# Two tiles of layer two's first chunk take their denominators by tokens, and two chunks' sums of phi(K) leave TensorE

## The chip, the cores and the metric

The kernel runs on one core of one Trainium2 chip. The metric is the device time of one execution in microseconds. The engines are TensorE (PE, with its weight loads as PEld), VectorE (DVE), ScalarE (ACT), GpSimd (POOL) and SyncE (SP), which only issues DMAs. Each engine works through its own instructions in order and waits for the others by semaphores.

## The reference

Two layers of the same weights: linear attention and an MLP, each behind a layer norm and with a residual. There are 2048 tokens of 512 values, 32 heads of 16 values, and 1792 hidden values.

```python
def _A_ref(x, wqkv, wo):
    qkv = (x @ wqkv) ...            # q, k, v: heads x tokens x 16
    phi = lambda t: jnp.where(t > 0, t + 1, jnp.exp(t)) + 1e-6
    pq, pk = phi(q), phi(k)
    kv = jnp.einsum("bhsd,bhse->bhde", pk, v)
    z = jnp.einsum("bhsd->bhd", pk)
    num = jnp.einsum("bhqd,bhde->bhqe", pq, kv)
    den = jnp.einsum("bhqd,bhd->bhq", pq, z)[..., None] + 1e-6
    return (num / den)... @ wo
def _B_ref(x, w1, b1, w2, b2):
    return _gelu(_layernorm(x) @ w1 + b1) @ w2 + b2
x = A_x
x = x + _A_ref(_layernorm(x)); x = x + _B_ref(x)
x = x + _A_ref(_layernorm(x)); x = x + _B_ref(x)
```

## The kernel before

The tokens are cut into 4 chunks of 512, and each chunk into 4 tiles of 128 tokens (tile numbers 0 to 15). Names of operations end in layer, chunk or tile, and part: `K0_5` is the K projection of tile 5 in layer one, `Q1_0_2` the Q projection of chunk 0, part 2, in layer two.

Per tile: `stats`, `aggr`, `veps`, `pow` and `norm` make the layer norm (`A` before the attention, `B` before the MLP), a DMA transpose issued by SP (`TA`, `TB`) turns it, and `K` projects it. `exp`, `relu`, `min` and `phi` are the four steps of phi: two on ScalarE, `min` on VectorE, the last addition on VectorE or GpSimd. `G` collects y^T phi(K) over the tokens (y being the normed input; four PSUM banks are held for it in layer one, `gacc` adds chunks up in layer two). `KV` multiplies that by Wv, `kvm` masks it to the diagonal blocks of the heads, `M` multiplies by Wo, and `cpm` copies the result to `gtb`, the matrix that `WO` uses. Then come `RA` (residual), the second norm, `W1` with the gelu, `W2`, and `RB` (residual) or the output `OD`. `b2` adds the MLP's bias to the residual beside that.

In layer one tiles 0 to 3 are turned by TensorE (`PTC0`, `PTC1`, `PTA0_2`, `PTA0_3`, copied by ScalarE as `tcC`, `tcA`). In the first microseconds TensorE runs filler matmuls (`warm`).

The sum z of phi(K) over all tokens is made in two ways in `attn_z`. One takes 16 matmuls of one column per chunk (`Z0_c`, L970; `zs` adds them up). The other, used for the first three chunks of layer two, adds the tiles' phi(K) elementwise in fp32 (`za`, L958), splits the sum into two bf16 halves (`zhi`, `zlo`) and sums each over the tokens with four matmuls of one column (`ZH`, L933 and L934; `zsh` takes the result).

The denominators are made in two ways in `attn_den`. By features: Q is made with features on the partitions, `D` (L1100) multiplies it by `zb` (z on the heads' diagonal blocks), ScalarE takes Ln and Exp(-x) (L1102, L1104) and `pr` multiplies (L1108). By tokens: Q is made with tokens on the partitions, `pz` multiplies by the row of z (L1077), `red` sums per head (L1080), `den` adds 1e-6 (L1083, 128x32 values), `rec` is the reciprocal (L1085), `pr` multiplies (L1089), and a DMA transpose `TP` (L1093) turns the result. Chunk 0 of each layer goes by features, the others by tokens.

The order on every engine is written out by name in `CONF["ORDER"]`, the buffers in `PLACES`, and in `WAY` which engine does a step that several can do. `LOADS` gives the first loads and their queues. There is no scheduler at run time: each engine takes its list from first to last.

Of the kernel before, what the change touches and what calls it, by code (L numbers as in the profile page):

```python
# [1359 lines left out]
```

## Time and profile before

| | us |
|---|---|
| median of 3 runs | 323.17 (322.78 to 323.9) |
| the profiled execution | 323.1 |
| its span, first to last instruction | 321.9 |
| busy: PE, DVE, ACT, POOL | 318.0, 218.1, 189.3, 145.5 |
| granted TensorE clock | 1.000 |

Lines of a timeline read: start in us, length in us, engine, line of the source, operation, output <- input, shape, how many were merged, and in brackets the idle time of the engine before it and what ended that. Lines of waits read: who waited <- for whom: us in total, times, longest. Groups read: busy us, mean ns of one | idle before. Lines of one source line read: shortest/median/longest in ns, first and last start. DMA lines read: how many, (KB each,) median us from issue to landing. Rows of windows read: stretch and its length, then busy us (count) of PE, PEld, DVE, ACT and POOL, granted clock, DMA share and GB/s.

### The profile page before, as it was taken

How to read it: one execution, taken by the hardware profiler on the slowest of the kernel's cores; microseconds unless marked ns; L12 is line 12 of the kernel's file. 1: busy time of each engine (PE TensorE's matmuls, PEld its weight loads, DVE VectorE, ACT ScalarE, POOL GpSimd, SP SyncE). 2: the span in 40 equal slices, each digit the busy share in tenths (PEclk: the TensorE clock that was granted, in tenths of full speed). 3: DMA queues.
4: the chain of work that ended last, by engine and by line, in shares of the span. 5: the costliest groups of instructions: out<-in, count | busy, mean ns of one | idle time of the engine just before them, and what ended most of it. 6: DMA issues, size and time to landing. Idle time of an engine off the chain costs nothing.

```text
span 321.9 us, 4748 instructions
## 1 busy us (share of the span) xinstructions
PE 318.0 (99%) x1703; PEld 157.4 (49%) x1703; DVE 218.1 (68%) x529; ACT 189.3 (59%) x324; POOL 145.5 (45%) x216
## 2 busy tenths in 40 slices
PE   8999999999999999999999999999999999999997
PEld 3444554666444444444444444558544444444444
DVE  5998789999786774028848899999889881101103
ACT  5898656797730636667962367979634442663320
POOL 6573978688655355101822415887454163000000
DMA  7844793142121412111010200122232322201002
GB/s 257 200 81 85 241 348 85 35 82 36 33 49 34 82 33 51 34 33 32 18 40 10 51 16 0 35 51 52 50 62 54 98 65 67 49 0 35 16 33 65
DMA packets 52355, 21.68 MB, mean 67 GB/s; under 512 B 47532, under 2 KB 50860, under 8 KB 52332
## 3 DMA queue, kind: packets, MB, share of 16 engines
q1 hardware_dynamic: 50844, 16.37, 22.4%
q0 software_dynamic: 1056, 4.72, 4.3%
q10 hardware_dynamic: 432, 0.30, 0.3%
q8 instruction: 13, 0.21, 0.3%
q14 instruction: 10, 0.08, 0.1%
HBM read 8.00 MB, written 2.10 MB: 31 GB/s over the span
## 4 chain that ended last, share of the span: by engine, by line
PE 97%; DMA 2%; DVE 0%; issue 0%
PE ps L1153 30%; PE ps L1190 29%; PE ps L1123 9%; PE ps L879 8%; PE ps L896 6%; PE ps L984 4%; PE ps L1013 4%; DMA t<-in_A_x_dram 2%; PE ps L909 2%; PE ps L1176 1%; PE ps L970 1%; PE ps L1034 1%; PE ps L1057 1%; PE ps L1100 1%; DVE stats L775 0%; PE ps L1048 0%
## 5 line engine op out<-in xcount | busy, mean ns | idle before, releaser
L1158 ACT ACTIVATE gT<-ps,b1c 128x512 bf16<-128x512 f32 (+1 forms) x140 | 77.0, 601 | 68.7 <-PE ps L1153 68.1
L1153 PE MATMUL ps<-t,w 128*128 128x512 bf16 (+1 forms) x560 | 102.5, 336 | 0.0
L1190 PE MATMUL ps<-w,gT 128*128 128x512 bf16 x434 | 98.6, 379 | 0.0
L1153 PEld LDWEIGHTS ps<-t,w 128*128 128x128 bf16 x560 | 54.8, 98 | 43.7 <-ACT gT L1158 0.2
L1190 PEld LDWEIGHTS ps<-w,gT 128*128 128x128 bf16 x434 | 42.5, 98 | 50.4
L784 POOL TENSOR_TENSOR rstd<-veps,neghalf 128x1 f32<-128x1 f32 x64 | 39.0, 625 | 41.1 <-DVE veps L782 38.9
L847 ACT ACTIVATE eb<-ps 128x512 bf16<-128x512 f32 x62 | 35.4, 606 | 19.3 <-PE ps L896 7.3
L1200 DVE TENSOR_TENSOR yb<-ps,xsb 128x512 bf16<-128x512 f32 x15 | 10.2, 688 | 41.4 <-PE ps L1190 41.4
L775 DVE BATCH_NORM_STATS2 stats<-xsb 128x6 f32<-128x512 f32 x48 | 32.0, 681 | 0.3
L1123 PE MATMUL ps<-gtb,t 128*128 128x512 bf16 x128 | 31.4, 379 | 0.0
L879 PE MATMUL ps<-wqkv,t 128*128 128x512 bf16 x128 | 30.9, 379 | 0.3 <-ACT t L835 0.3
L858 ACT ACTIVATE rb<-ps 128x512 bf16<-128x512 f32 x43 | 25.3, 607 | 5.8 <-PE ps L879 5.8
L798 ACT ACTIVATE yb<-xsb,nmr,rstd 128x512 bf16<-128x512 f32 x21 | 16.9, 814 | 15.1 <-POOL nmr L795 15.1
L896 PE MATMUL ps<-wqkv,t 128*128 128x512 bf16 x96 | 24.1, 379 | 0.0
L1089 POOL TENSOR_TENSOR t<-t,rr 128x512 bf16<-128x512 bf16 x18 | 19.3, 1072 | 9.0 <-DVE rr L1085 6.4
L782 POOL TENSOR_SCALAR veps<-mv 128x1 f32<-128x1 f32 x35 | 8.2, 236 | 32.7 <-DVE mv L777 31.3
L1196 DVE TENSOR_TENSOR xsb<-ps,xsb 128x512 f32<-128x512 f32 x16 | 10.8, 678 | 17.9 <-PE ps L1190 17.9
L1139 POOL TENSOR_TENSOR xsb<-xsb,b2b 128x512 f32<-128x512 f32 x17 | 21.4, 1267 | 3.0 <-DVE yb L803 2.9
L1077 POOL TENSOR_TENSOR lr<-t,zrow 128x512 f32<-128x512 bf16 x14 | 16.5, 1179 | 7.3 <-ACT zrow L997 4.5
L1123 PEld LDWEIGHTS ps<-gtb,t 128*128 128x128 bf16 x128 | 12.5, 98 | 14.5
L803 DVE TENSOR_SCALAR yb<-xsb,mv,rstd 128x512 bf16<-128x512 f32 x27 | 14.5, 542 | 7.3 <-POOL rstd L784 6.0
L879 PEld LDWEIGHTS ps<-wqkv,t 128*128 128x128 bf16 x128 | 12.1, 98 | 14.7 <-ACT t L835 0.9
(99 smaller groups left out, 363.7 us busy)
## 6 DMA issues: line engine op xcount, KB each, us to landing
w<-in_B_w_dram POOLq DMA_DIRECT2D x4, 896.0 KB, 9.1
out_dram<-yb SPq DMA_DIRECT2D x15, 128.0 KB, 2.0
...
t<-yb SPq DMA_TRANSPOSE x62, 2.5
...
t<-in_A_x_dram SPq DMA_DIRECT2D x1, 384.0 KB, 3.3
```

Of the source, the lines that this page charges most:

```text
L775: G.op("dve", lambda e: e.bn_stats(stats[:, s.slot, :], src()), 620, reads=src_keys, writes=[k + "s"], tiles=[s, *src_tiles], name=f"stats ...
L784: G.op("pool", lambda e: e.tensor_tensor(rstd[:, s.slot:s.slot + 1], veps[:, s.slot:s.slot + 1], neghalf[:], op=ALU.pow), 570, reads=[k + ...
L847: G.op("act", lambda e: e.activation(eb[:, et.slot, :], bank(bt), ACT.Exp, scale=by()), 478, reads=[src_key, *more_keys], writes=[f"e{tag} ...
L858: G.op("act", lambda e: e.activation(rb[:, rt.slot, :], bank(bt), ACT.Relu, scale=by()), 478, reads=[src_key, *more_keys], writes=[f"r{tag ...
L879: ins = e.matmul(bank(b), lhsT=yTa(yT)[:, dt, k * P:(k + 1) * P], rhs=wqkv[:, dt, D:2 * D], start=(i == 0 and n == 0), stop=(i == len(part ...
L896: ins = e.matmul(bank(b), lhsT=yTa(yT)[:, dt, k * P:(k + 1) * P], rhs=wqkv[:, dt, 0:D], start=(dt == 0), stop=(dt == DT - 1))
L1089: lambda e, d=d, tok=tok, heads=heads: e.tensor_tensor(heads(tok()), heads(tok()), rr[:, d.slot, :].unsqueeze(2).broadcast_to([P, H, DH]), ...
L1123: ins = e.matmul(bank(wb), lhsT=yTa(pq)[:, kt, k * P:(k + 1) * P], rhs=gtb[:, kt, :], start=(kt == 0), stop=(kt == DT - 1))
L1139: G.op("pool" if on_pool else "dve", lambda e: e.tensor_tensor(xsb[:, st, :], xsb[:, st, :], b2b[:], op=ALU.add), 1120 if on_pool else 600 ...
L1153: ins = e.matmul(bank(b, n), lhsT=w1[:, dt, ft * P:(ft + 1) * P], rhs=yTa(yT)[:, dt, k0 * P:k1 * P], start=(dt == 0), stop=(dt == DT - 1))
L1158: G.op("act", lambda e, ft=ft, b=b, k0=k0, k1=k1, n=n: e.activation(gT[:, g.slot, ft * 512 + k0 * P:ft * 512 + k1 * P], bank(b, n), ACT.Ge ...
L1190: ins = e.matmul(bank(b), lhsT=gT[:, g.slot, ft * 512 + k * P:ft * 512 + (k + 1) * P], rhs=w2[:, ft, :], start=(ft == 0), stop=(ft == FT - 1))
```

## The change

Four parts:

1. Layer two, chunk 0 (`"den1_0": "half"`): tiles 0 and 1 keep the denominators by features, on 256 columns (names ending in `c`: `Q1_0_0c`, `D1_0_0c`, `ln1_0_0c`, ...), and tiles 2 and 3 go by tokens (`Q1_0_2`, `pz1_0_2`, ..., `TP1_0_2`).
2. Layer one, chunks 0 and 1 (`"zc0": "0 1"`): phi(K) is added up elementwise (`zaA1` to `zaA7`, of which `zaA2` on VectorE and six on GpSimd), split (`zhiA`, `zloA`), and summed by `ZHA`; `Z0_0` and `Z0_1` go.
3. `LOADS`: tiles 1 to 3 of chunk 0 (`x1`) are loaded by ACT's queue in place of SP's; the K weights' quarters are used in the order 0, 2, 1, 3 in place of 2, 0, 3, 1.
4. `ORDER`, `PLACES` and `WAY` are new throughout. 13 more of the bias additions `b2` stand on VectorE in place of GpSimd. The filler's amount is the same.

The loops also learn to take the chunks in a given order (`CHUNKS`), which is 0, 1, 2, 3 everywhere, and a load of half a tile that isn't used.

```diff
-    LOADS=[['x0', 'sp', 'x', 0, 0, 1, ''], ['x1', 'sp', 'x', 0, 1, 4, ''], ['wkb', 'act', 'wk', 0, 2, 3, 'ones'], ['wka', 'sp', 'wk', 0, 0, 1, ''], ['wkd', 'act', 'wk', 0, 3, 4, ''], ['wkc', 'sp', 'wk', 0, 1, 2, ''],
...
+    LOADS=[['x0', 'sp', 'x', 0, 0, 1, ''], ['wka', 'sp', 'wk', 0, 0, 1, ''], ['wkc', 'sp', 'wk', 0, 1, 2, ''], ['x1', 'act', 'x', 0, 1, 4, 'ones'], ['wkb', 'act', 'wk', 0, 2, 3, ''], ['wkd', 'act', 'wk', 0, 3, 4, ''],
...
# ORDER, "dve":
-... statsA0_5 normA0_3 aggrA0_5 normA0_1 statsA0_4 mink0_0 ...
+... statsA0_4 normA0_1 aggrA0_4 normA0_3 statsA0_7 mink0_0 ...
-... red0_1_0 red0_1_1 kvm0_2 den0_1_1 kvm0_0 kvm0_1 kvm0_3 cpm0_2 ...
+... red0_1_0 red0_1_1 kvm0_2 kvm0_1 kvm0_0 den0_1_0 kvm0_3 cpm0_2 ...
-... gt1_0 den1_1_2 rec1_1_2 gt1_3 red1_1_1 kvm1_2 kvm1_0 kvm1_3 kvm1_1 den1_1_0 den1_1_1 cpm1_0 ...
+... gt1_0 rec1_0_2 gt1_3 rec1_1_2 red1_0_3 kvm1_3 kvm1_1 kvm1_0 den1_0_3 kvm1_2 rec1_0_3 cpm1_0 ...
# ORDER, "pe":
-... Z0_3 Q0_0_3 Z0_2 G0_8_0 G0_9_0 D0_0_2 G0_10_0 D0_0_0 ...
+... Z0_3 G0_8_0 Z0_2 Q0_1_1 ZHA G0_9_0 D0_0_2 D0_0_0 G0_10_0 ...
-... KV0_3 Q0_2_1 M0_2 M0_0 M0_1 Q0_2_2 M0_3 Q0_2_3 WO0_0_0 ...
+... KV0_3 Q0_2_1 M0_2 M0_1 Q0_2_3 M0_0 M0_3 Q0_2_2 WO0_0_0 ...
# WAY
-        "den0_3": "tok", "den1_1": "tok", "den1_2": "tok", "den1_3": "tok", "ks0": "2|0|3|1",
+        "den0_3": "tok", "den1_0": "half", "den1_1": "tok", "den1_2": "tok", "den1_3": "tok", "ks0": "0|2|1|3",
+        "za9": "pool", "zaA2": "dve", "zc0": "0 1",
...
-        def by_token(L, c):
-            return eng(f"den{L}_{c}") == "tok"
+        def by_token(L, c, k=0):
+            way = eng(f"den{L}_{c}")
+            return way == "tok" or (way == "half" and k >= 2)
+
+        def by_half(L, c):
+            return eng(f"den{L}_{c}") == "half"
...
 def attn_q(L, c, yT, pq):
+            half = by_half(L, c)
+            own = pq
+            if half:
+                own = tokq[(L, c)] = Tile(T4, f"pqt{L}_{c}")
+            n = 2 * P if half else 4 * P
+            if not by_token(L, c):
+                for kt in range(DT):
+                    b = Tile(psum, f"q{L}_{c}_{kt}" + "c" * half, "q")
...
+                            ins = e.matmul(bank(b, n), lhsT=wqkv[:, dt, kt * P:(kt + 1) * P], rhs=yTa(yT)[:, dt, 0:n],
+                                           start=(dt == 0), stop=(dt == DT - 1))
...
+            for k in range(4):
+                if by_token(L, c, k):
                     b = Tile(psum, f"q{L}_{c}_{k}", "q")
...
 def attn_den(L, c, pq):
+            half = by_half(L, c)
+            src = tokq[(L, c)] if half else pq
+            pt = pq if half or not by_token(L, c) else Tile(T4, f"pt{L}_{c}")
+            n = 2 * P if half else 4 * P
...
+                    G.op("pe", lambda e, kt=kt, b=b: e.matmul(bank(b, n), lhsT=zb[:, kt * P:(kt + 1) * P], rhs=yTa(pq)[:, kt, 0:n], start=True, stop=True),
+                         MM if n == D else n / 2.4 + 2.5, reads=[key, "zb"], writes=[f"d{tag}"], tiles=[b, pq], name=f"D{tag}", lat=MM_DRAIN)
...
+            for k in range(4):
+                if not by_token(L, c, k):
+                    continue
+                tag = f"{L}_{c}_{k}"
...
```

More of the change, by code (lines that the diff above doesn't have):

```diff
@@ L709, in load_w, with load_half @@
                                [f"{which}_{d}" for d in range(d0, d1)], name=name, kb=128 * (d1 - d0), after=after)
+        def load_half(name, queue, h, after):
+            G.parts[("x0", 0)] = (("x0", 0, 0), ("x0", 0, 1))
+            ps_ = slice(64 * h, 64 * h + 64)
+            loaded[name] = dma(queue, lambda e: e.dma_start(
+                t4[ps_, x0[0].slot, 0:D].rearrange("p (k d) -> p k d", k=1), rows(x_dram, 0)[ps_, 0:1, :]),
+                [("x0", 0, h)], [x0[0]], name=name, kb=64, after=after)
         for name, queue, what, at, lo, hi, behind in cf["LOADS"]:
             after = [loaded[b] for b in behind.split()]
-            if what == "x":
+            if what == "half":
+                load_half(name, queue, at, after)
+            elif what == "x":
                 load_x(name, queue, at, lo, hi, after)
@@ L854, in phi @@
                                                              op0=ALU.add, op1=ALU.max),
-                     600, reads=[f"e{tag}", src_key], writes=[dst_key], tiles=[et, bt, *dst_tiles], name=f"phi{tag}", lat=90)
+                     600 if n == D else 330, reads=[f"e{tag}", src_key], writes=[dst_key], tiles=[et, bt, *dst_tiles], name=f"phi{tag}", lat=90)
                 return
             rt = Tile(RB, f"r{tag}")
-            G.op("act", lambda e: e.activation(rb[:, rt.slot, :], bank(bt), ACT.Relu, scale=by()), 478, reads=[src_key, *more_keys],
+            G.op("act", lambda e: e.activation(rb[:, rt.slot, 0:n], bank(bt, n), ACT.Relu, scale=by()), 478 if n == D else 265, reads=[src_key, *more_keys],
@@ L859, in phi @@
                  writes=[f"r{tag}"], tiles=[bt, rt, *more_tiles], name=f"relu{tag}", lat=90)
-            G.op("dve", lambda e: e.tensor_scalar(eb[:, et.slot, :], eb[:, et.slot, :], 1.0, 1e-6, op0=ALU.min, op1=ALU.add),
-                 210, reads=[f"e{tag}"], writes=[f"e{tag}"], tiles=[et], name=f"min{tag}", lat=80, fast=True)
+            G.op("dve", lambda e: e.tensor_scalar(eb[:, et.slot, 0:n], eb[:, et.slot, 0:n], 1.0, 1e-6, op0=ALU.min, op1=ALU.add),
+                 210 if n == D else 120, reads=[f"e{tag}"], writes=[f"e{tag}"], tiles=[et], name=f"min{tag}", lat=80, fast=True)
@@ L900, in attn_q, with attn_z @@
                          tiles=[b, yT], name=f"Q{L}_{c}_{k}", lat=MM_DRAIN, n=4)
-                    phi(b, f"q{L}_{c}_{k}", lambda k=k: t4[:, pq.slot, k * D:(k + 1) * D], f"pq{L}_{c}_{k}", [pq],
+                    phi(b, f"q{L}_{c}_{k}", lambda k=k: t4[:, own.slot, k * D:(k + 1) * D], f"pq{L}_{c}_{k}", [own],
                         f"q{L}_{c}_{k}")
-                return
-            for kt in range(DT):
-                b = Tile(psum, f"q{L}_{c}_{kt}", "q")
-                def fn(e, kt=kt, b=b):
-                    for dt in range(DT):
-                        ins = e.matmul(bank(b), lhsT=wqkv[:, dt, kt * P:(kt + 1) * P], rhs=yTa(yT)[:, dt, :],
-                                       start=(dt == 0), stop=(dt == DT - 1))
-                    return ins
-                G.op("pe", fn, 4 * MM, reads=[f"yT{L}_{4 * c + k}" for k in range(4)] + ["wq"], writes=[f"q{L}_{c}_{kt}"],
-                     tiles=[b, yT], name=f"Q{L}_{c}_{kt}", lat=MM_DRAIN, n=4)
-                phi(b, f"q{L}_{c}_{kt}", lambda kt=kt: yTa(pq)[:, kt, :], f"pq{L}_{c}_{kt}", [pq], f"q{L}_{c}_{kt}")
         zfirst = {}
-        def attn_z(L, c, pks):
-            by_sum = [int(v) for v in (eng("zc0") or "").split()] if L == 0 else list(range(NC - 1))
+        def attn_z(L, c, pks, order):
+            by_sum = [int(v) for v in (eng("zc0") or "").split()] if L == 0 else order[:NC - 1]
+            others = [v for v in order if v not in by_sum]
             def fold(add):
@@ L973, in attn_z, with attn_g_held @@
             G.op("pe", fn, 400, reads=[f"pk{L}_{4 * c + k}" for k in range(4)] + ["onesm"], writes=[f"zc{L}_{c}"], tiles=[b, *pks], name=f"Z{L}_{c}", lat=MM_DRAIN, n=16)
-            total(b, f"zc{L}_{c}", f"zs{L}_{c}", bool(L) or c != min(v for v in range(NC) if v not in by_sum))
-            if L == 0 and by_sum and c == max(v for v in range(NC) if v not in by_sum):
+            total(b, f"zc{L}_{c}", f"zs{L}_{c}", bool(L) or c != others[0])
+            if L == 0 and by_sum and c == others[-1]:
                 fold(True)
-        def attn_g_held(L, st, k, y, ykey, pk, gb):
-            parts = [(dc,) for dc in range(DT)] if st == ST - 1 else [tuple(range(DT))]
+        def attn_g_held(L, st, k, y, ykey, pk, gb, first, last):
+            parts = [(dc,) for dc in range(DT)] if last else [tuple(range(DT))]
             for part in parts:
@@ L984, in fn @@
                         ins = e.matmul(ps[:, gb.slot + dc, :], lhsT=yb[:, y.slot, dc * P:(dc + 1) * P], rhs=pkb[:, pk.slot, :],
-                                       start=(st == 0), stop=(st == ST - 1))
+                                       start=first, stop=last)
                     return ins
                 keys = [f"g{L}_{dc}" for dc in part]
-                G.op("pe", fn, len(part) * MM, reads=[ykey, f"pk{L}_{st}"] + (keys if st else []), writes=keys,
+                G.op("pe", fn, len(part) * MM, reads=[ykey, f"pk{L}_{st}"] + ([] if first else keys), writes=keys,
                      tiles=[y, pk, gb], name=f"G{L}_{st}_{part[0]}", lat=MM_DRAIN, n=len(part))
@@ L1004, in attn_g_out, with attn_g_chunk @@
                 copy(gtb[:, dc, :], gb, f"g{L}_{dc}", ("gt", dc), dc % 2, f"g{L}_{dc}", off=dc)
-        def attn_g_chunk(L, c, ys, ykeys, pks):
+        def attn_g_chunk(L, c, ys, ykeys, pks, first, last):
             for dc in range(DT):
@@ L1042, in attn_kv @@
                  reads=["zs", "bdmask"], writes=["zb"], name=f"zb{L}", lat=40, fast=True)
-            if any(by_token(L, c) for c in range(NC)):
+            if any(by_token(L, c, 3) for c in range(NC)):
                 zr = Tile(psum, f"zr{L}", "t")
@@ new lines, in attn_den @@
+            half = by_half(L, c)
+            src = tokq[(L, c)] if half else pq
+            pt = pq if half or not by_token(L, c) else Tile(T4, f"pt{L}_{c}")
+            n = 2 * P if half else 4 * P
+            if not by_token(L, c):
+                for kt in range(DT):
+                    tag = f"{L}_{c}_{kt}" + "c" * half
+                    b = Tile(psum, f"d{tag}", "n")
+                    r = Tile(LR, f"lr{tag}")
+                    key = f"pq{L}_{c}_{kt}" + "c" * half
+                    G.op("pe", lambda e, kt=kt, b=b: e.matmul(bank(b, n), lhsT=zb[:, kt * P:(kt + 1) * P], rhs=yTa(pq)[:, kt, 0:n], start=True, stop=True),
+                         MM if n == D else n / 2.4 + 2.5, reads=[key, "zb"], writes=[f"d{tag}"], tiles=[b, pq], name=f"D{tag}", lat=MM_DRAIN)
+                    G.op("act", lambda e, b=b, r=r: e.activation(lr[:, r.slot, 0:n], bank(b, n), ACT.Ln, bias=eps6[:]), 575 if n == D else 362,
+                         reads=[f"d{tag}", "eps6"], writes=[f"l{tag}"], tiles=[b, r], name=f"ln{tag}", lat=90, table="exp")
+                    G.op("act", lambda e, r=r: e.activation(lr[:, r.slot, 0:n], lr[:, r.slot, 0:n], ACT.Exp, scale=-1.0), 536 if n == D else 323,
+                         reads=[f"l{tag}"], writes=[f"l{tag}"], tiles=[r], name=f"rec{tag}", lat=110, table="exp")
@@ L1093, in attn_den @@
-                    dma("sp", lambda e, k=k, tok=tok: e.dma_start_transpose(yTa(pt)[:, :, k * P:(k + 1) * P], tok()), [f"pt{tag}"],
-                        tiles=[pq, pt], reads=[f"pq{tag}"], name=f"TP{tag}", sem=("pT", pq, k), transpose=True)
-                return pt
-            for kt in range(DT):
-                b = Tile(psum, f"d{L}_{c}_{kt}", "n")
-                r = Tile(LR, f"lr{L}_{c}_{kt}")
-                tag = f"{L}_{c}_{kt}"
-                G.op("pe", lambda e, kt=kt, b=b: e.matmul(bank(b), lhsT=zb[:, kt * P:(kt + 1) * P], rhs=yTa(pq)[:, kt, :], start=True, stop=True),
-                     MM, reads=[f"pq{tag}", "zb"], writes=[f"d{tag}"], tiles=[b, pq], name=f"D{tag}", lat=MM_DRAIN)
-                G.op("act", lambda e, b=b, r=r: e.activation(lr[:, r.slot, :], bank(b), ACT.Ln, bias=eps6[:]), 575,
-                     reads=[f"d{tag}", "eps6"], writes=[f"l{tag}"], tiles=[b, r], name=f"ln{tag}", lat=90, table="exp")
-                G.op("act", lambda e, r=r: e.activation(lr[:, r.slot, :], lr[:, r.slot, :], ACT.Exp, scale=-1.0), 536,
-                     reads=[f"l{tag}"], writes=[f"l{tag}"], tiles=[r], name=f"rec{tag}", lat=110, table="exp")
+                         lambda e, kt=kt, r=r: e.tensor_tensor(yTa(pq)[:, kt, 0:n], yTa(pq)[:, kt, 0:n], lr[:, r.slot, 0:n], op=ALU.mult),
@@ new lines, in attn_den, with attn_out @@
+                     1150 if on_pool else 600, reads=[f"rr{tag}", f"pq{tag}"], writes=[f"pq{tag}"], tiles=[d, src],
+                     name=f"pr{tag}", lat=60, fast=not on_pool)
+                dma("sp", lambda e, k=k, tok=tok: e.dma_start_transpose(yTa(pt)[:, :, k * P:(k + 1) * P], tok()), [f"pt{tag}"],
+                    tiles=[src, pt], reads=[f"pq{tag}"], name=f"TP{tag}", sem=("pT", src, k), transpose=True)
+            return pt
+        def attn_out(L, c, k, pq, base, base_keys, base_tiles, first):
@@ L1116, in attn_out @@
             st = 4 * c + k
             wb = Tile(psum, f"wo{L}_{st}", "w")
-            parts = [(kt,) for kt in range(DT)] if st == 0 else [tuple(range(DT))]
+            parts = [(kt,) for kt in range(DT)] if first else [tuple(range(DT))]
             for part in parts:
@@ L1206, in build_kernel @@
         gb = Tile(psum, "g4", "g4", 4)
-        pq1, trs = [], []
-        for c in range(NC):
+        pq1, trs = {}, []
+        orders = cf["CHUNKS"]
+        for c in orders[0]:
             yT = Tile(T4, f"yT0_{c}")
             pq = Tile(T4, f"pq0_{c}")
-            pq1.append(pq)
+            pq1[c] = pq
             pks = []
@@ L1252, in build_kernel @@
         for L in range(2):
-            nxt = []
-            for c in range(NC):
+            nxt = {}
+            chunks = orders[1 + L]
+            for c in chunks:
                 yT = Tile(T4, f"yBT{L}_{c}")
@@ L1269, in build_kernel @@
                     pq = Tile(T4, f"pq1_{c}")
-                    nxt.append(pq)
+                    nxt[c] = pq
                 ys, ykeys, pks = [], [], []
```

102 lines of the change are left out of this document (50 added, 52 removed), and 530 rows, old and new, of tables (ORDER, PLACES, WAY).

## The prediction

> **What bounds the kernel now.** I read the page first (busy time, the slices, the chain that ended last), then the waits of TensorE, then the timelines of TensorE, VectorE and GpSimd around each place that the change touches.
>
> ```profile
> span 321.9 us, 4748 instructions
> ...
> PE 318.0 (99%) x1703; PEld 157.4 (49%) x1703; DVE 218.1 (68%) x529; ACT 189.3 (59%) x324; POOL 145.5 (45%) x216
> ...
> PE   8999999999999999999999999999999999999997
> ...
> PE 97%; DMA 2%; DVE 0%; issue 0%
> ```
> ```profile
> PE ps L749 <- PEq L1345: 0.8, 1, 0.8
> PE ps L825 <- DVE yb L803: 0.5, 1, 0.5
> PE ps L879 <- ACT t L835: 0.3, 1, 0.3
> PE ps L825 <- DVE yb L789: 0.2, 1, 0.2
> ```
>
> The second block is the whole list of TensorE's waits: 1.8 us, all in the head. From 9.39 us on TensorE never waits. So the time is the head, plus the matmuls one behind the other, plus a tail. An instruction taken off TensorE is worth its spacing; any other step costs nothing until TensorE has to wait for it. The profiled execution took 323.1 us, 1.2 more than its span; the median of the runs, 323.17, is 0.07 above it.
>
> **TensorE's own work.** A matmul's duration overlaps the next one's, so I price by start to start.
>
> ```profile
> 28.80 0.54 PE L970 MATMUL ps<-onesm,pkb 128*128 128x1 bf16 x16
> 29.20 0.59 PE L879 MATMUL ps<-wqkv,t 128*128 128x512 bf16 x2
> ...
> 38.63 0.38 PE L1100 MATMUL ps<-t,zb 128*128 128x512 bf16 x1
> ...
> 189.24 0.17 PE L933 MATMUL ps<-onesm,dz 128*128 128x1 bf16 x1
> ...
> 189.44 1.89 PE L1013 MATMUL ps<-pkb,yb 128*128 128x512 bf16 x8
> ```
> ```profile
> 60.62 5.68 PE ps L1153 x52
> 66.30 1.51 PE ps L1190 x7
> ```
>
> The sums of phi(K) of chunks 0 and 1 (Z0_0 and Z0_1, 16 matmuls of one column each) go: 2 x 0.40 = 0.80. ZHA comes, eight of one column as layer two has them at 189.24: 0.20. The four D1_0 matmuls go from 512 columns (0.216, as 1.51/7) to 256 (5.68/52 = 0.109): 4 x 0.107 = 0.43. The Q matmuls of that chunk become 16 of 256 columns and 8 of 512 in place of 16 of 512: 1.74 + 1.73 against 3.46, nothing. Together **-1.03 us**. The added instructions on the other engines are covered or not as follows. I laid out the new order of every engine, instruction by instruction, with durations and hand-over times of the trace; the old order laid out so gives its span within 0.1 us.
>
> **The head.**
>
> ```profile
> 4.60 0.63 ACT L766 ACTIVATE eb<-t 128x512 bf16<-128x512 bf16 x1 [2.52 <-DMA t<-in_A_x_dram]
> ...
> 8.09 0.69 DVE L775 BATCH_NORM_STATS2 stats<-t 128x6 f32<-128x512 bf16 x1 [0.72 <-DMA t<-in_A_x_dram]
> 8.70 0.40 DVE L803 TENSOR_SCALAR yb<-t,stats,rstd 128x512 bf16<-128x512 bf16 x1
> 9.02 0.17 DVE L777 BATCH_NORM_AGGREGATE mv<-stats 128x2 f32<-128x6 f32 x1
> 9.11 0.38 DVE L803 TENSOR_SCALAR yb<-t,mv,rstd 128x512 bf16<-128x512 bf16 x1
> ...
> 9.16 0.40 PE L825 MATMUL ps<-idp,yb 128*128 128x128 bf16 x4 [0.47 <-DVE yb L803]
> 9.39 1.89 PE L879 MATMUL ps<-wqkv,t 128*128 128x512 bf16 x8
> ```
>
> VectorE stands at the statistics that wait for chunk 1's load (8.09). Behind them before comes normA0_3 (8.70), whose transpose PTA0_3 releases TensorE at 9.16. After, normA0_1 and aggrA0_4 stand between the two: 9.11 - 8.70 = **+0.41 us**. If chunk 1's load lands 0.4 sooner, the cost is gone; 0.4 later doubles it. Tiles 1 to 3 of chunk 0 (x1) leave from ACT's queue instead of SP's:
>
> ```profile
> 1.48 0.86 ACTq L708 DMA_DIRECT2D wqkv<-in_A_wqkv_dram  x2
> ```
> ```profile
> t<-in_A_x_dram SPq DMA_DIRECT2D x1, 384.0 KB, 3.3
> ```
>
> At 1.48 + 3.3 they land at 4.8 instead of 4.6. ScalarE's sum (4.60) waits for them and the copy tcC0, for which K0_0 waits, is queued behind it, so K0_0 starts 0.2 later. This is hidden: TensorE stands before PTA0_3 anyway, with 0.7 us to spare. Only a landing after about 5.4 would cost, up to 0.4 at 5.8. I take nothing.
>
> **The denominators of layer one.** ZHA reads the split of the added-up phi(K), and zb, which D0_0_2 needs, now hangs on it.
>
> ```profile
> 37.08 0.36 DVE L941 TENSOR_TENSOR zs<-ps,zs 128x4 f32<-128x4 f32 x2 [0.77 <-PE ps L970]
> 37.48 0.69 DVE L1040 TENSOR_TENSOR zb<-bdmask,zs 128x512 bf16<-128x512 bf16 x1
> ```
>
> Before, zb ended at 38.17 and D0_0_2 started at 38.63. After, the chain from ZHA's start is 0.34 (its last matmul starts 0.17 in and takes 0.17), 0.18 (zshA), 0.69 (zb) and three hand-overs of 0.03 to 0.04 (37.48 behind 37.44): 1.31 us. TensorE has ZHA itself (0.20) and one G of four matmuls (4 x 0.216 = 0.86) to do in that time: 1.06. So D0_0_2 waits **+0.24**. Zero if the adds end early enough; 0.5 if VectorE is held once in it.
>
> **Short VectorE steps behind GpSimd.** This is the part that the diff does not tell.
>
> ```profile
> 203.35 2.38 POOL L1108 TENSOR_TENSOR t<-t,lr 128x512 bf16<-128x512 bf16 x2
> ...
> 204.03 0.60 DVE L1083 TENSOR_SCALAR rd<-rd 128x32 f32<-128x32 f32 x2
> ```
> ```profile
> L1083 DVE TENSOR_SCALAR rd<-rd x24: 117/172/517, 43.3 to 246.2; 128x32 f32<-128x32 f32 x24
> ```
> ```profile
> 47.11 1.06 POOL L1089 TENSOR_TENSOR t<-t,rr 128x512 bf16<-128x512 bf16 x1
> 48.12 1.16 POOL L1077 TENSOR_TENSOR lr<-t,zrow 128x512 f32<-128x512 bf16 x1
> ...
> 47.81 0.28 DVE L1053 TENSOR_TENSOR kvb<-ps,bdmask 128x128 bf16<-128x128 f32 x1
> 48.01 0.19 DVE L1083 TENSOR_SCALAR rd<-rd 128x32 f32<-128x32 f32 x1
> 48.12 0.67 DVE L1053 TENSOR_TENSOR kvb<-ps,bdmask 128x128 bf16<-128x128 f32 x3
> ```
> ```profile
> 49.88 0.38 PE L1057 MATMUL ps<-wo,kvb 128*128 128x512 bf16 x1
> ```
>
> The small den step takes 0.12 to 0.17 us, but 0.517 at 204.03, where GpSimd's product ran until about 204.5; the masks from PSUM (L1053) run beside GpSimd unhindered. The Trainium skill states the rule in SBUF — State Buffer, section "SBUF: two separate sides": VectorE and GpSimd share one port pair as an exclusive lock, and whichever starts second is fully blocked. By that rule the trace agrees: 0.517 against 0.172. Without it the next two terms would be 0.06 each. At 48.01 the old order was lucky: the den step fell where one product ended (48.17). The new order puts den0_1_0 between kvm0_0 and kvm0_3; on my layout GpSimd is in the product pr0_1_3 from 48.6 to 49.7, den0_1_0 comes at 48.7 and is held 0.9. kvm0_3 ends at 50.0 instead of 48.8, so M0_3 (49.88 before) waits 0.07; cpm0_2 ends at 50.6 instead of 49.5, and Q0_2_2, which needs the bank that it empties, waits 0.38; M0_2 waits 0.06 for red0_1_1 in front of kvm0_2. **+0.51**, between 0.06 (the den step falls into a gap) and about 1.1 (a whole GpSimd operation).
>
> **Layer two, chunk 0.** Tiles 3 and 4 get token denominators: two of pz, red, den, rec, pr and a transpose each. The feature half keeps four exp, relu, min, add, Ln, Exp and products of 256 columns.
>
> ```profile
> L1158 ACT ACTIVATE gT<-ps,b1c 128x256 bf16<-128x256 f32 x56 | 23.4, 474 | 16.6 <-PE ps L1153 16.2
> ```
>
> No row has these at 256 columns; the nearest, the gelu, takes 0.474. They feed WO1_0, where my layout leaves 0.02 to 0.2 us of cover; if each took its 512-column time, the price is 0.2 or so. red1_0_2, red1_0_3 and their den steps are queued on VectorE between the gt adds and the masks: gt1_3 comes 0.06 late for KV1_3, and den1_0_3, held 0.28 behind a product, stands before kvm1_2, which M1_2 needs: 0.27. **+0.33**, bounds 0 and 0.9.
>
> The two extra transposes on SP's queue run ahead of TB1_0 and TB1_1; the layout leaves TB1_1 0.17 us before W11 needs it. The 13 bias additions (b20, b21) that move from GpSimd to VectorE run beside MLP matmuls, with VectorE at 68% overall: nothing, at worst 0.3.
>
> **Sum.** -1.03 + 0.41 + 0.24 + 0.51 + 0.33 = +0.46: 323.1 + 0.46 = 323.6, and 323.63 from the median. I forecast **323.6**, own range 322.9 to 324.1.
>
> **The rivals.** *The gain comes through.* GpSimd's phase is a few tenths off and the den steps fall into its gaps. Then the terms 0.51 and 0.33 are gone: 323.1 - 0.38 = 322.7; with the head also hidden (chunk 1's load 0.4 sooner) 322.3, and with D0_0_2 on time 322.1. For it: GpSimd's pace is uncertain to 0.2 us. Against it: that its operations follow each other almost without gap around 48 (47.11 to 49.28).
>
> *GpSimd's adds hold VectorE in layer one.*
>
> ```profile
> 8.00:36.00 28.00, 27.53 (x174) 12.88 (x172) 25.43 (x76) 25.21 (x47) 16.52 (x38) 1.00 0.54 121
> ```
> ```profile
> L958 POOL TENSOR_TENSOR zacc<-zacc,pkb x4: 1156/1158/1337, 157.5 to 179.4; 128x512 f32<-128x512 f32 x4
> ```
>
> Six of the seven new adds (zaA) go to GpSimd, 1.16 each, in a stage where VectorE works 25.43 of 28 us. If each holds a VectorE step for half its length, that is 3.5 us against 2.6 idle, 0.9 more than fits: 324.5. It decides once a phi(K) step is held beyond the cover of its G. My layout has a step held three times there, by 0.4 to 1.0, without reaching TensorE. [...] *A transpose lands late.*
>
> ```profile
> t<-yb SPq DMA_TRANSPOSE x62, 2.5
> ```
> ```profile
> t<-yb SPq DMA_TRANSPOSE x1, 3.3
> ```
>
> The second row is the transposes issued between 216.0 and 217.4, a single one, against the median of all. If TB1_1 takes 3.3, W11 waits 0.6; TA0_4, with 0.18 us to spare, can cost another 0.2: 324.4. That the change would not do what it says is out: the built program has the 24 fewer one-column matmuls and D1_0 at 256 columns.
>
> **How the numbers follow.** Forecast 0.48, gain through 0.20 (half of it below 322.2), adds 0.18, late transposes 0.14. A measurement can tell 0.3%, 0.97 us, from no change. Faster by more needs 322.2 or less: 0.10. Slower by more needs over 324.14, where the last two cases lie: 0.32. The rest, 0.58, is within. The range leaves out a tenth at each end: 322.3 to 324.7.
>
> **What would show it.** Right: K0_2 starts near 9.8 instead of 9.39; TensorE's waits name zb before L1100's successor by 0.2, kvb and gtb around 49 to 51 and 204; L1083's longest is near 1 us; the D1_0 matmuls are 0.11 apart. Wrong: TensorE's waits behind the head sum to under 0.3 (the gain comes through), or above 1.8 with the waits before K, G or W11.

## The result, and the profile after

The changed kernel takes **325.62 us** (median of 6 runs, 325.32 to 327.32) against 323.62 for the kernel before in the same set: ratio 1.0076, interval 1.0056 to 1.0096, so 1.8 to 3.1 us slower. The prediction was 323.6 with 324.7 as its upper end.

The first profiled execution, of 327.32 us, was the slowest of the six. Two lines of its page:

```profile
span 326.1 us, 4741 instructions
...
PE 86%; POOL 6%; DVE 4%; ACT 2%; DMA 1%; issue 1%; DVEq 0%; POOLq 0%
```

The second line is the chain that ended last: before, TensorE held 97% of it, and now GpSimd and VectorE have a tenth. A second profile of the same kernel (run e7_after, span 325.1) has these waits of TensorE:

```profile
PE ps L1183 <- ACT gT L1188: 1.0, 1, 1.0
PE ps L763 <- PEq L1377: 0.8, 1, 0.8
PE ps L899 <- ACT t L855: 0.4, 1, 0.4
PE ps L899 <- ACT eb L867: 0.4, 1, 0.4
PE ps L899 <- DVE pkb L873: 0.3, 1, 0.3
PE ps L932 <- ACT eb L867: 0.3, 1, 0.3
PE ps L845 <- DVE yb L823: 0.2, 1, 0.2
```

Before, every wait of TensorE lay in the first 9.4 us. Now W1 (L1183), K (L899) and Q (L932) wait as well. In the changed kernel's lines L802 is `veps`, L804 `pow`, L815 `nmr`, L818 the norm on ScalarE, L823 the norm on VectorE, L867 to L884 the steps of phi, L983 the adds `zaA`, L1009 `G`, L1130 `den`, L1169 `b2`. A row shows less idle time than a matmul was late, since a matmul's row lasts 0.38 us and the next starts 0.216 behind it; lateness below is taken from start to start.

Summed so over e7_after, the matmuls were late by 2.18 us between 20 and 34 us (Q0_1_3 0.45, K0_12 0.08, K0_14 0.29, K0_10 0.56, K0_8 0.50, K0_11 0.31), 1.15 at W10_0_2_1, 0.26 at D0_0_2, 0.36 at M0_2 and Q0_2_2, 0.26 in layer two (Z1_3, M1_2, W11_0_10_0). With the -1.03 of TensorE's work that is +3.2, and the span is 3.2 above before's 321.9. The prediction named waits above 1.8 us before K, G or W11 as a sign of being wrong; they came before K and Q, and one before W1.

### The profile page after: what moved, and what is told of

It reads as the page before. It is cut to its first block, busy times and chain, and to the rows that moved or that the text cites. A ratio compares the mean times of both kernels' runs of the same rounds, so it can differ in the third digit from the quotient of the medians.

```text
span 326.1 us, 4741 instructions
## 1 busy us (share of the span) xinstructions
PE 320.4 (98%) x1687; PEld 157.7 (48%) x1687; DVE 231.7 (71%) x556; ACT 191.2 (59%) x330; POOL 139.7 (43%) x211
## 4 chain that ended last, share of the span: by engine, by line
PE 86%; POOL 6%; DVE 4%; ACT 2%; DMA 1%; issue 1%; DVEq 0%; POOLq 0%
PE ps L1183 30%; PE ps L1220 29%; PE ps L1153 8%; PE ps L899 5%; PE ps L932 5%; PE ps L1038 4%; DMA t<-in_A_x_dram 1%; POOL rstd L804 1%; POOL zacc L983 1%; PE ps L1206 1%; PE ps L920 1%; DVE yb L823 1%; POOL lr L1124 1%; POOL t L1106 1%; POOL w L742 1%
## 5 line engine op out<-in xcount | busy, mean ns | idle before, releaser
L1183 PE MATMUL ps<-t,w 128*128 128x512 bf16 (+1 forms) x560 | 102.4, 336 | 0.0
L1183 PEld LDWEIGHTS ps<-t,w 128*128 128x128 bf16 x560 | 54.6, 98 | 43.8 <-ACT eb L867 0.4
L804 POOL TENSOR_TENSOR rstd<-veps,neghalf 128x1 f32<-128x1 f32 x64 | 39.8, 629 | 34.5 <-DVE veps L802 31.7
L867 ACT ACTIVATE eb<-ps 128x512 bf16<-128x512 f32 (+1 forms) x64 | 35.8, 589 | 18.4 <-DVE t L884 6.6
L878 ACT ACTIVATE rb<-ps 128x512 bf16<-128x512 f32 (+1 forms) x45 | 25.5, 586 | 17.2 <-PE ps L899 9.4
L899 PE MATMUL ps<-wqkv,t 128*128 128x512 bf16 x128 | 33.3, 387 | 2.3 <-ACT t L855 1.3
L1136 POOL TENSOR_TENSOR t<-t,rr 128x512 bf16<-128x512 bf16 x18 | 19.3, 1080 | 18.4 <-DVE rr L1132 13.7
L932 PE MATMUL ps<-wqkv,t 128*128 128x512 bf16 x104 | 26.2, 379 | 0.4 <-ACT eb L867 0.3
L818 ACT ACTIVATE yb<-xsb,nmr,rstd 128x512 bf16<-128x512 f32 x21 | 16.9, 809 | 15.4 <-POOL nmr L815 15.3
L1169 DVE TENSOR_TENSOR xsb<-xsb,b2b 128x512 f32<-128x512 f32 x28 | 18.8, 688 | 4.8 <-ACT yb L818 4.8
L884 POOL TENSOR_TENSOR pkb<-eb,rb 128x512 bf16<-128x512 bf16 x5 | 5.9, 1178 | 37.2 <-ACT rb L878 28.6
L899 PEld LDWEIGHTS ps<-wqkv,t 128*128 128x128 bf16 x128 | 12.1, 99 | 18.8 <-ACT t L855 2.3
L1124 POOL TENSOR_TENSOR lr<-t,zrow 128x512 f32<-128x512 bf16 x15 | 17.7, 1189 | 5.4 <-ACT zrow L1022 2.9
```

What stands on the lines that cost most here:

```text
L804: G.op("pool", lambda e: e.tensor_tensor(rstd[:, s.slot:s.slot + 1], veps[:, s.slot:s.slot + 1], neghalf[:], op=ALU.pow), 570, reads=[k + ...
L867: G.op("act", lambda e: e.activation(eb[:, et.slot, 0:n], bank(bt, n), ACT.Exp, scale=by()), 478 if n == D else 265, reads=[src_key, *more ...
L878: G.op("act", lambda e: e.activation(rb[:, rt.slot, 0:n], bank(bt, n), ACT.Relu, scale=by()), 478 if n == D else 265, reads=[src_key, *mor ...
L899: ins = e.matmul(bank(b), lhsT=yTa(yT)[:, dt, k * P:(k + 1) * P], rhs=wqkv[:, dt, D:2 * D], start=(i == 0 and n == 0), stop=(i == len(part ...
L932: ins = e.matmul(bank(b), lhsT=yTa(yT)[:, dt, k * P:(k + 1) * P], rhs=wqkv[:, dt, 0:D], start=(dt == 0), stop=(dt == DT - 1))
L1124: lambda e, r=r, tok=tok: e.tensor_tensor(lr[:, r.slot, :], tok(), zrow[:], op=ALU.mult), 1150 if on_pool else 600,
```

## The experiments

**The head.** In the first profile x1 landed at 5.98 us, the first K waited for it, and TensorE ran at half pace. Its rows, then those of e7_after:

```profile
5.11 0.85 PE L763 MATMUL ps<-const-bfloat16-1.0 128*128 128x256 bf16 x3
7.26 0.61 PE L899 MATMUL ps<-wqkv,t 128*128 128x512 bf16 x1 [1.31 <-ACT t L855]
...
10.18 1.03 PE L899 MATMUL ps<-wqkv,t 128*128 128x512 bf16 x4
```
```profile
5.08 0.49 PE L763 MATMUL ps<-const-bfloat16-1.0 128*128 128x256 bf16 x3
6.01 0.39 PE L899 MATMUL ps<-wqkv,t 128*128 128x512 bf16 x1 [0.44 <-ACT t L855]
...
9.14 0.40 PE L845 MATMUL ps<-idp,yb 128*128 128x128 bf16 x4 [0.24 <-DVE yb L823]
```

Three 256-column matmuls last 0.85 there and 0.49 here, a K matmul 0.61 and 0.39; the last transpose of the head, at 9.14 here, stands at 11.04 there. My first theory (theory 1) made this head the loss; theory 2 took GpSimd's adds.

```diff
# e1_loads_back: the changed kernel with the loads of before; e4_before_new_loads: the reverse, on the kernel before
-['x1', 'act', 'x', 0, 1, 4, 'ones']  ... "ks0": "0|2|1|3"
+['x1', 'sp', 'x', 0, 1, 4, '']  ... "ks0": "2|0|3|1"
```

> The changed kernel with the first loads of before: tiles 1 to 3 of chunk 0 on SP's queue again, the K weights' quarters in their old order. Theory 1 (the late first load costs the head 1.3 us of waiting, and with it a slow TensorE in the first 12 us): x1 lands near 4.6 in place of 6.0, the first K waits under 0.1 us for the copy tcC0, G0_0_0 starts near 11.5 in place of 13.2, and the time falls by 1.3 to 2.0 us against the changed kernel (ratio 0.994 to 0.996). Theory 2 (GpSimd's adds in layer one are the whole loss, and a late start only hands them more cover): the time stays within 0.4 us of the changed kernel, since the stalls between 23 and 36 us grow by what the head gains.

> The kernel before with nothing but the changed kernel's first loads (tiles 1 to 3 of chunk 0 on ACT's queue, the K weights' quarters used in the order 0, 2, 1, 3). Theory 1: x1 lands near 6.0, the first K starts near 7.3 in place of 5.9, and the time rises by 1.0 to 1.7 us (ratio 1.003 to 1.005). If the prediction's 'I take nothing' holds: within 0.3 us of the kernel before.

> The changed kernel once more, unaltered, for a second look at its head: in the first profiled execution tiles 1 to 3 of chunk 0 landed at 5.98 us and TensorE ran its 256-column matmuls 0.21 us apart until 10.2 us. Theory 2 (GpSimd's adds in layer one are the loss, the slow head was of that execution alone): the load lands near 5.0, the first K starts near 6.3, G0_0_0 within 0.6 us of before's 11.1, and the span is about 324.2, with the same waits between 20 and 34 us (2.2 us). Theory 1 (the head is part of the loss): the head is as in the first profile and the span is near 326.

Measured: e1 325.84 us (ratio to before 1.0088, 1.0069 to 1.0107), no faster than the changed kernel. e4 323.32 against 323.28 (1.0008, 0.9997 to 1.0018). e7 had its load at 4.73, G0_0_0 at 11.10 (before 11.12) and the same waits between 20 and 34 us. Its span, 325.1, is 0.9 above the 324.2 that theory 2 had expected, since a wait that the first profile did not have (W10_0_2_1, below) came in. Theory 1 falls: the slow head belonged to that execution. It comes again, though: of ten profiled executions with x1 on ACT's queue, x1 landed between 4.73 and 5.98, G0_0_0 started between 11.0 and 13.2, and two ran at half pace until 10 us; of six with x1 on SP's queue it landed between 4.49 and 4.69 and G0_0_0 started between 10.9 and 11.5.

**The sums of phi(K) back on TensorE, at a bad place.**

```diff
# e2_z_back: the changed kernel with
-"zc0": "0 1",      # no zaA, zhiA, zloA, ZHA, zshA
+# pe: "... G0_3_0 Z0_0 ..." and "... K0_12 Z0_1 ..."
# e3_both_back: this, and the loads of e1
```

> The changed kernel with the sums of phi(K) of chunks 0 and 1 on TensorE again (Z0_0 and Z0_1 back: 0.80 us; the seven adds, the split and ZHA gone: 0.20 us less). Theory 2 (the adds on GpSimd hold VectorE's and GpSimd's small steps and cost TensorE 2.2 us of waits between 23 and 36 us, and D0_0_2 another 0.26): these waits fall under 0.5 us and the time falls by 2.0 + 0.26 - 0.6 = 1.3 to 1.7 us against the changed kernel. Theory 1 (only the head costs): TensorE gets 0.6 us more to do and the time rises by 0.3 to 0.6 us.

> Both undone: the first loads and the two sums as before; what is left of the change is the half denominators of layer two (-0.43 us of TensorE) and the new orders with the den step behind GpSimd (+0.51) and layer two's waits (+0.33). If the prediction's later terms hold: 0.4 to 0.9 us above the kernel before. If the waits there are what the changed kernel's trace shows (Q0_2_2 0.30, M0_2 0.07, layer two 0.28): 0.2 to 0.3 above plus the head's order, 0.4. If the two first causes add up without touching each other, it is e1's gain and e2's gain together below the changed kernel, within 0.4 us.

Measured: 332.97 us and 333.72, 7 to 8 us slower than the changed kernel, as neither theory had it. The trace of e2: two waits of TensorE, and the windows around them (PE, PEld, DVE, ACT and POOL busy, then the granted clock):

```profile
PE ps L929 <- DVE t L807: 3.4, 1, 3.4
PE ps L833 <- DVE zs L900: 1.6, 1, 1.6
```
```profile
20.00:25.00 5.00, 1.61 (x20) 0.95 (x22) 4.34 (x14) 1.42 (x4) 1.60 (x6) 0.95 0.29 55
25.00:30.00 5.00, 5.00 (x18) 1.97 (x17) 0.31 (x3) 3.80 (x7) 0.00 (x0) 0.71 0.26 52
```

I had put Z0_0 into the PSUM bank that q0_1_0 leaves, and its last reader ends at 23.3 us. From 25 to 30 us, behind the 3.4 us wait, the granted clock was 0.71 on average. So these two runs tell of the place and not of the sums, as e9 shows next.

**The sums at a good place, the adds left out, the adds moved.**

```diff
# e9_z_tensor: as e2, but
+# pe: "... Q0_0_2 Z0_0 ..." (bank of q0_0_0), "... K0_14 Z0_1 ..." (bank of k0_12)
# e8_no_adds: the changed kernel with
+                    if L == 0 and st >= 3:
+                        continue
# e10_adds_behind: the changed kernel with, on GpSimd,
-... zaA4 powA0_10 nmrA0_10 zaA5 vepsA0_8 ... powA0_9 zaA6 zaA7
+... powA0_10 nmrA0_10 vepsA0_8 ... powA0_9 zaA4 zaA5 zaA6 zaA7
```

> The changed kernel with the sums of chunks 0 and 1 on TensorE again, as in the run e2_z_back, but at places where TensorE need not wait for them: Z0_0 behind Q0_0_2 in the bank that q0_0_0 leaves, Z0_1 behind K0_14 in the bank that k0_12 leaves. Theory 2: the waits of 2.2 us and D0_0_2's 0.26 go, TensorE gets 0.6 more: 1.6 to 2.0 us below the changed kernel, so within 0.5 us of the kernel before. If e2's 8 us came from the sums themselves and not from their place, this run is several us slower than the changed kernel as well.

> The changed kernel without five of the seven adds of phi(K) in layer one (zaA3 to zaA7 on GpSimd are left out, so z lacks tiles 3 to 7); every order is otherwise the same, and TensorE has the same matmuls. Theory 2: TensorE's waits between 20 and 34 us (2.2 us) fall under 0.4 us, and the time falls by 1.8 to 2.2 us against the changed kernel. If the waits come from the new orders of the other engines and not from the adds: no change, within 0.4 us.

> The changed kernel with two of GpSimd's adds (zaA4, zaA5) moved behind its last small step of the layer norms (powA0_9), so that zaA4 to zaA7 follow each other. It tells two ways apart in which the adds can cost. Queue (the adds stand in GpSimd's order ahead of the small steps that ScalarE's and VectorE's norms wait for): the waits of K0_10, K0_8 and K0_14 go and the time falls by 0.8 to 1.5 us. Port (VectorE's two-input and normalizing steps are held while an add runs): the holds only move to the steps that run beside the four adds, K0_9 or K0_14 waits 0.8 to 1.5 us for a phi(K) or phi(Q) step, and the time is within 0.5 us of the changed kernel or above it.

Measured: e9 324.40 us (1.0035, 1.0020 to 1.0050), 1.2 below the changed kernel's first median and 1.8 below e7's 326.18. All the waits between 20 and 34 us are gone in its trace. It stays 1.1 above the kernel before, where at most 0.5 was expected; its trace has W10_0_2_1 late by 1.00 and K0_4 by 0.33. e10 took 327.52 us: the waits of K0_14 and K0_10 went, those of K0_8 (0.60) and K0_11 (0.30) stayed, and K0_9 got a new one of 1.00:

```profile
35.13 1.04 PE L833 MATMUL ps<-wqkv,t 128*128 128x512 bf16 x4 [0.84 <-DVE pkb L807]
```

So both ways cost: the adds' place in GpSimd's queue, and the steps of VectorE that they hold. How much each takes, e10 does not tell; its first K was late as well (x1 at 5.52). In e8 the waits between 20 and 34 us fell from 2.18 to 0.72, but the time, 325.85, is only 0.3 below e7's and 0.2 above the first median, where a gain of 1.8 to 2.2 was expected. Its profiled execution had one of the two slow heads (G0_0_0 at 12.4); the other four have no profile, so why they were no faster stays open. That left the price of the adds open, and the pair e15 and e16 below settles it.

**One small step back on VectorE.** The wait at W10_0_2_1, 1.00 to 1.15 us, was in six of the eight profiles with `vepsB0_6` on GpSimd. VectorE, then GpSimd, then TensorE of e7_after:

```profile
69.11 0.42 DVE L884 TENSOR_TENSOR t<-eb,rb 128x512 bf16<-128x512 bf16 x1
69.45 0.29 DVE L880 TENSOR_SCALAR eb<-eb 128x512 bf16<-128x512 bf16 x1
69.65 0.68 DVE L1169 TENSOR_TENSOR xsb<-xsb,b2b 128x512 f32<-128x512 f32 x1
70.25 0.69 DVE L1124 TENSOR_TENSOR lr<-t,zrow 128x512 f32<-128x512 bf16 x1
70.86 0.68 DVE L1127 TENSOR_REDUCE rd<-lr 128x32 f32<-128x512 f32 x1
```
```profile
68.87 2.12 POOL L802 TENSOR_SCALAR veps<-mv 128x1 f32<-128x1 f32 x1
```
```profile
77.75 0.61 PE L1183 MATMUL ps<-t,w 128*128 128x256 bf16 x4 [0.99 <-ACT gT L1188]
```

A step of 128 values lasts 2.12 us and ends as VectorE comes to its reduction. The norm on ScalarE waits for it, and behind that norm stand two exponentials of phi(Q) between two table loads, and then the gelu that W10_0_2_1 waits for. The third row is b20_3, a bias addition that the change moved to VectorE. In the first profile the same step got through:

```profile
71.04 0.38 POOL L802 TENSOR_SCALAR veps<-mv 128x1 f32<-128x1 f32 x1
```

```diff
# e11_veps_back: the changed kernel with
-"vepsB0_6": "pool"
+"vepsB0_6": "dve"      # behind aggrB0_6, as before
```

> The changed kernel with one small step moved back: vepsB0_6 (128x1) on VectorE as before, in place of GpSimd. In the second profile of the changed kernel this step lay 2.12 us on GpSimd, beside a row of VectorE steps without a gap (phi, min, b20_3, pz), and W10_0_2_1 waited 1.15 us at 77.7 us for the gelu behind the norm that needs it. Starved (VectorE's row holds GpSimd's step): that wait goes and the time falls by 0.8 to 1.2 us against the changed kernel, to 324.6 or so. If the wait has another cause (ScalarE's two table loads there, or the norm's place in ScalarE's order), it stays and the time is the same within 0.3 us.

Measured: the wait is gone in the trace. The forecast gain of 0.8 to 1.2 did not show: the time is 325.74 us (324.96 to 327.12), which can't be told from the changed kernel's. In the profiled execution x1 landed at 5.88, and W11_0_10_0 waited 0.72 for TB1_1. That last wait is of the same kind. `powB1_1` in e11, then in e7_after:

```profile
213.72 1.47 POOL L738 TENSOR_TENSOR rstd<-veps,neghalf 128x1 f32<-128x1 f32 x1
```
```profile
213.83 0.77 POOL L804 TENSOR_TENSOR rstd<-veps,neghalf 128x1 f32<-128x1 f32 x1
```

**Undoing the causes together.**

```diff
# e12_three_back: e9, vepsB0_6 on VectorE, and on VectorE
-... kvm1_0 den1_0_3 kvm1_2 ...
+... kvm1_0 kvm1_2 den1_0_3 ...
# e13_three_xc2: e12, and on SP's queue
-... TA0_1 xc2 TA0_4 ...
+... TA0_1 TA0_4 xc2 ...
# e14_loads_too: e12, the loads of e1, and vepsB1_1 on VectorE
# e15_adds_alone: e14, but with the adds zaA1 to zaA7 and ZHA for the two sums
# e16_adds_out: e15 with the lines of e8
```

> Three parts undone at once: the sums of chunks 0 and 1 on TensorE as in e9_z_tensor, vepsB0_6 on VectorE, and den1_0_3 behind kvm1_2 in place of before it. Half denominators of layer two, first loads, bias additions and the orders stay changed. If the causes add up: e9's 324.4, less 1.0 for W10_0_2_1, less 0.1 for M1_2: 323.3, within 0.3 of the kernel before, since the half denominators' 0.43 are then spent on K0_4 (0.33 in e9) and Z1_3 (0.07). If another wait takes the place of the removed ones: 324 or more.

> e12_three_back with the load xc2 issued behind the transpose TA0_4 on SP's queue in place of ahead of it. If TA0_4 lands late in e9 because it shares the queues with xc2, K0_4's wait of 0.33 us goes and the time falls by another 0.3, below the kernel before by 0.2 to 0.4 us. If it is late because its norm is: no change; if xc2 then lands too late for the statistics at 21 us: slower by up to 1 us.

> e12_three_back with two parts more undone: the first loads of before (tiles 1 to 3 of chunk 0 on SP's queue, K weights' quarters in the old order) and vepsB1_1 on VectorE. On ACT's queue those tiles landed between 4.7 and 6.0 us in ten profiled executions, on SP's at 4.6 to 4.7 in three. If the late landings cost on average what the heads of the profiles show (0.3 to 0.5 us), the time falls from 323.6 to about 323.2, the kernel before within 0.3 us. If ACT's queue costs nothing on average, as e4 had it: 323.5 to 323.7 again. Faster than before by more than 0.3 us is expected by neither.

> The changed kernel with everything undone that was found to cost, but for the adds: the first loads of before, vepsB0_6 and vepsB1_1 on VectorE, den1_0_3 behind kvm1_2. It differs from e14_loads_too only in the sums of chunks 0 and 1 (adds on GpSimd, split and ZHA in place of Z0_0 and Z0_1). If the adds cost what the waits say: 2.2 us between 20 and 34 us, 0.26 at D0_0_2, 0.35 at M0_2 and Q0_2_2, less 0.6 of TensorE and less K0_4's 0.3: 1.9 us above e14's 323.6, so 325.5. If they cost nothing in time: 0.6 below e14, 323.0.

> e15_adds_alone without five of the seven adds (zaA3 to zaA7 are left out, z lacks tiles 3 to 7). If the adds are the cause: TensorE's waits between 20 and 34 us fall from 2.2 to 0.7 us, as in e8_no_adds, and the time falls by 1.3 to 1.6 us, to about 324.0. If the new orders are: the time stays within 0.4 us of e15.

| run | median us | ratio to before, interval |
|---|---|---|
| e12_three_back | 323.59 | 1.0010, 0.9996 to 1.0024 |
| e13_three_xc2 | 323.96 | 1.0032, 1.0019 to 1.0045 |
| e14_loads_too | 323.58 | 1.0014, 0.9995 to 1.0032 |
| e15_adds_alone | 325.47 | 1.0071, 1.0042 to 1.0100 |
| e16_adds_out | 323.69 | 1.0020, 1.0002 to 1.0039 |

e12 is 0.8 below e9, as the waits of vepsB0_6 and M1_2 are gone; a new one took part of it, W10_1_13_0 0.82 for the transpose TB0_4, which landed 4.5 us behind its issue (median of all 2.5). e13 gained nothing by xc2's place: K0_4's wait was gone in e12's profile already. e14 is no better than e12, so the loads cost nothing that these runs can tell. e15 came out at the 325.5 that the adds' theory expected, and e16 fell by a little more than its 1.3 to 1.6: the adds zaA3 to zaA7 alone cost 325.47 - 323.69 = 1.78 us, and all seven with ZHA, against the sums on TensorE, 325.47 - 323.58 = 1.89 (1.8 by the ratios). Between G0_6_0 and G0_7_0 stand the same 24 matmuls of 512 columns (24 x 0.216 = 5.18 us). TensorE's rows in e15, then in e16:

```profile
28.21 1.03 PE L943 MATMUL ps<-pkb,yb 128*128 128x512 bf16 x4
29.37 1.04 PE L833 MATMUL ps<-wqkv,t 128*128 128x512 bf16 x4
30.79 1.04 PE L833 MATMUL ps<-wqkv,t 128*128 128x512 bf16 x4 [0.39 <-ACT eb L801]
32.15 3.08 PE L833 MATMUL ps<-wqkv,t 128*128 128x512 bf16 x12 [0.32 <-DVE pkb L807]
35.06 1.03 PE L943 MATMUL ps<-pkb,yb 128*128 128x512 bf16 x3
```
```profile
28.36 1.03 PE L945 MATMUL ps<-pkb,yb 128*128 128x512 bf16 x4
29.22 4.48 PE L833 MATMUL ps<-wqkv,t 128*128 128x512 bf16 x20
33.54 1.03 PE L945 MATMUL ps<-pkb,yb 128*128 128x512 bf16 x3
```

6.85 us with the adds, 5.18 without: no wait is left in this stretch. Between 20 and 34 us 1.88 of lateness falls to 0.45, all of it at Q0_1_3. The busy time of 20 to 34 us in e15 and in e16 (PE, PEld, DVE, ACT, POOL):

```profile
20.00:34.00 14.00, 12.97 (x57) 4.96 (x56) 12.52 (x34) 12.04 (x23) 11.05 (x18) 1.00 0.37 75
```
```profile
20.00:34.00 14.00, 13.66 (x63) 6.03 (x64) 12.46 (x38) 13.65 (x26) 6.38 (x14) 1.00 0.37 76
```

VectorE is as busy in both. GpSimd's 11.05 fall to 6.38, and ScalarE gets more done in the same stretch. How the adds reach TensorE is seen in e7_after: GpSimd's rows, then ScalarE's norms and one of VectorE's.

```profile
22.82 0.76 POOL L804 TENSOR_TENSOR rstd<-veps,neghalf 128x1 f32<-128x1 f32 x1
23.68 0.26 POOL L815 TENSOR_SCALAR nmr<-mv,rstd 128x1 f32<-128x1 f32 x1
23.91 1.16 POOL L983 TENSOR_TENSOR zacc<-zacc,pkb 128x512 f32<-128x512 f32 x1
25.15 0.44 POOL L802 TENSOR_SCALAR veps<-mv 128x1 f32<-128x1 f32 x1
25.68 0.71 POOL L804 TENSOR_TENSOR rstd<-veps,neghalf 128x1 f32<-128x1 f32 x1
26.49 0.26 POOL L815 TENSOR_SCALAR nmr<-mv,rstd 128x1 f32<-128x1 f32 x1
```
```profile
26.79 0.81 ACT L818 ACTIVATE yb<-t,nmr,rstd 128x512 bf16<-128x512 bf16 x1 [0.54 <-POOL nmr L815]
28.29 0.81 ACT L818 ACTIVATE yb<-t,nmr,rstd 128x512 bf16<-128x512 bf16 x1 [0.21 <-POOL nmr L815]
```
```profile
30.01 1.31 DVE L823 TENSOR_SCALAR yb<-t,mv,rstd 128x512 bf16<-128x512 bf16 x1
```

GpSimd works almost without gap until 31 us. The small steps (veps, pow, nmr) that the norms wait for stand behind the adds. ScalarE waits for them, and the exponentials behind its norms come late. VectorE's norm, 0.41 us elsewhere, is held to 1.31 beside zaA6 and zaA7. The chain that ended last in e7_after shows the way (start, length, what):

```profile
19.12 1.12 POOL zacc L983
...
28.29 0.02 ACT yb L818
...
29.01 0.58 ACT eb L867
...
30.09 1.23 DVE yb L823
...
33.15 1.90 PE ps L899 x8
```

From 18.6 to 28.3 us it runs through nothing but GpSimd's adds and small steps; of the stretch from 19 to 36 us the adds hold 20.0% and `pow` 19.3%. In e9, e12 and e14 the chain over this stretch is TensorE's own matmuls.

No version beats the kernel before. In e14 the half denominators still save their matmuls, but K0_4 waits 0.29, W10_1_13_0 0.38 (for TB0_4) and Z1_3 0.07, and the span is 322.0 against 321.9.

## Why the prediction was wrong

**TensorE's own work, -1.03: right as far as it is visible.** ZHA's matmuls stand 0.025 apart, and a D1_0 matmul is followed after 0.10:

```profile
202.28 0.27 PE L1098 MATMUL ps<-t,zb 128*128 128x256 bf16 x1
202.38 1.03 PE L1038 MATMUL ps<-pkb,yb 128*128 128x512 bf16 x4
```

**The head, +0.41 and "I take nothing" for x1: wrong in form.** In e7 the 0.41 did not come, since chunk 1's load landed at 7.66 in place of 8.07, the exception that the step named. x1 on ACT's queue landed at 4.73 to 5.98, not at a fixed 4.8, and above 5.5 it cost 0.6 to 1.0 us (e10, e11), where I had allowed 0.4. In the medians the loads cost nothing that can be measured (e4: at most 0.6).

**D0_0_2, +0.24: right,** 0.26 in e7.

**den0_1_0 behind GpSimd, +0.51: right in mechanism, 0.36 in size.** The step was held 0.94, against 0.9 of the layout; Q0_2_2 waited 0.31 and M0_2 0.06, M0_3 not at all. The longest `den` of e7 lasts 1.07, as the prediction said it would. In e7:

```profile
50.53 0.94 DVE L1130 TENSOR_SCALAR rd<-rd 128x32 f32<-128x32 f32 x1
```

**Layer two, +0.33: 0.19** (Z1_3 0.07, which the sum did not have, and M1_2 0.12 in place of 0.27; KV1_3's 0.06 did not come), and 0.07 for TB1_1. The tiles that the prediction calls 3 and 4 there are tiles 2 and 3. TB1_1 came 0.6 to 0.7 late in e1, e2, e3 and e11, the size that the rival of late transposes gave, but its norm was late, not its transpose: it landed 2.4 us behind its issue in all of them. That rival's late landing did occur at another place, TB0_4 in e12, e13 and e14.

**The adds: the step that failed.** The sum held no term for them: in the layout they held a VectorE step three times "without reaching TensorE". They stood among the rivals, at 0.9 us beyond what fits and a chance of 0.18. They cost 1.8 us of time (e15 against e16), and with five of them left out 1.4 to 1.5 us of the waits between 20 and 34 us go (2.18 to 0.72 in e8, 1.88 to 0.45 in e16). What is left is Q0_1_3's wait; it is gone in e9, e12 and e14, which have no add and Z0_0 back on TensorE, and which of the two ends it was not tried. I priced the adds by VectorE's idle time alone, and my layout, which is not shown here, gave GpSimd's small steps their shortest durations (pow 0.55, veps 0.19). In e7 between 20 and 29 us they last 0.6 to 0.8 and 0.4. By that layout GpSimd's queue was 1.7 us late by 28 us, and it was the queue that the norms waited for. So the rival had the place right and the way only in part: it counted the VectorE steps that are held, and the chain runs mostly through GpSimd's own.

**The bias additions, "nothing, at worst 0.3": no term of their own is shown, but the row that they joined cost.** I asked whether VectorE had room for them, not whom VectorE holds. One of them, b20_3, is one of the four VectorE steps that kept `vepsB0_6`, a 0.19 us step moved to GpSimd without a word of mine, for 2.1 us, and the wait behind it was 1.00 to 1.15 in most profiles. No run put b20_3 alone back. With `vepsB0_6` on VectorE again, e12 and e14 keep all the bias additions and stand at 1.0010 and 1.0014 of the kernel before.

The Trainium skill (SBUF — State Buffer, section "SBUF: two separate sides") says that a GpSimd operation shuts out a VectorE operation that runs in a 2-port mode or, where GpSimd reads SBUF too, has two SBUF inputs, and the other way round: whichever of the two starts first has the shared ports for its whole instruction. VectorE's norm agrees: 1.31 against 0.41, until the adds end. So does the step of phi that reads PSUM (L873), which ran beside an add at 28.45 for 0.69, no longer than alone. GpSimd's veps, 2.12 against 0.19, was held the other way, and for longer than one instruction. I had used the rule in one direction only.
